# The order of dimensions in the loads of q and the stores of the result of a linear-attention and feed-forward kernel

## The chip, the cores and the metric

The kernel runs on one core of a Trainium2 chip. The metric is the device time of one execution in microseconds, the median of several runs of the same program. A separate execution is recorded by the hardware profiler, and every view in this document comes from such an execution.

The core has five instruction streams that matter here. PE multiplies matrices (PEld is its loading of the stationary operand), DVE and ACT do elementwise work, POOL only sets constants, and SP issues almost all DMA transfers. SP is a queue: it issues in program order, and an issue that has to wait holds up everything behind it. The core's 16 DMA engines carry the transfers.

## The reference

```python
kv  = einsum('bhsd,bhse->bhde', k, v)            # per batch and head, 64 x 64
out = einsum('bhsd,bhde->bhse', q, kv)
rms = sqrt(mean(out * out, axis=-1) + 1e-6)
attn = out / rms * g_norm
x = attn.transpose(0, 2, 1, 3).reshape(4608, 512)  # tokens x (heads * 64)
h = x @ w_in                                     # 512 -> 2048
g = h * tanh(softplus(h))                        # mish
result = g @ w_out                               # 2048 -> 512
```

There are 8 batches, 8 heads, 576 positions and a head size of 64, all in float32; the two weights arrive in float64 and are converted on the chip.

## The kernel before

Both large products are done by a two-by-two block scheme with seven block products instead of eight. Each float32 operand is split into a high and a low part, and three matmuls stand for one.

**Part 1** goes over nine tiles of 512 tokens (j = 0 to 8). A tile is 28 slots: four groups of seven block products, each product 12 matmuls (`mm_in`, line 480). The products of tile j run while the attention of tile j + 1 is prepared in between, at slots that a table in `attention` fixes: `steps(u, n, ...)` puts a step at slot n of the tile before. A tile's attention has two units, u = 0 and u = 1, of four heads each. A unit loads q (`load`, line 288, into the tile `qs`, which has one buffer), transposes it in 32 by 32 blocks on DVE (`transpose`, line 293), splits it (lines 118 and 119), multiplies it with the batch's k-v product (`project`, lines 316 to 321), squares, sums and normalises. The load of u = 1 is put at slot 2 and its transpose at slot 7; the load of u = 0 of the next tile is put at slot 10, and its transpose at slot 28, which is slot 0 of the tile after.

A tile of 512 tokens straddles two batches of 576 positions, so it has one or two segments (`segments`). Tokens are placed so that a partition holds neighbouring positions: a segment of L * 32 positions of one head, which is contiguous in memory, is cut into 32 runs of L positions, and the 32-block transpose turns this into columns of tokens.

Evictions of the products go to the buffers `ula`, `ulb` and `ur` (two of each), through mish, and then to the scratch `gd` in HBM (`put_in`, lines 498, 503 and 506). A buffer can only be written again (lines 443, 448 and 457, on ACT) when its store has landed. Tile 0 also contains most of the k-v products: loads of k and v at lines 212 and 213, matmuls at line 233, and the copy at line 245. The conversion of w_in (line 135 loads it) falls there too, that of w_out in tiles 1 to 7.

**Part 2** multiplies g, read back from `gd` in 18 groups of 256 tokens (`g_load`, line 687, two groups ahead), with w_out (`mm_out`, line 728). A group's result of 256 rows stands in one `ur` buffer as [128 partitions, 2, 512]: token rows r = 0 in the first half, r = 1 in the second. `o_store` (line 752) writes it out after the group's last eviction (line 757).

What the change and the prediction touch: `load` in `unit_steps`, `o_store`, and the order of SP, which is the order of the plan's slots. The wait of ACT at line 448 for a landed `gd` store and that of DVE at line 293 for `qs` are the two places where DMA timing enters part 1.

Of the kernel before, what the change touches and what calls it, by code (L numbers as in the profile page):

```python
# [26 lines left out]
def linear_attention_rms_mish_ffn(  # L27
# [34 lines left out]
    nc = tc.nc  # L62
    B, H, S, D = q.shape
    NTOK, DM = out.shape
    DF = w_in.shape[1]
    w_in, w_out = w_in.bitcast(U32), w_out.bitcast(U32)
    P = 128
    R = 32
# [8 lines left out]
    G = 2 * P  # L77
# [183 lines left out]
    def segments(j):  # L261

        n = (S - T) * j
        segs = []
        if n:
            segs.append((j - 1, S - n, slice(0, n)))
        if n < T:
            segs.append((j, 0, slice(n, T)))
        return segs
# [3 lines left out]
    def unit_steps(j, u):  # L273
        st = {}

        def load():


            t = qs[u] = att.tile([P, 2, T // R * D], F32, name="qs")
            for a in range(2):  # L280
                for o in range(2):
                    for b, s0, cols in segments(j):
                        run = (cols.stop - cols.start) // R * D
                        src = q[b, 4 * u + 2 * a + o, s0:s0 + 1, :]
                        src = bass.AP(src.tensor, src.offset, [[R, 2], [run, R], [1, run - R]])
                        c0 = cols.start // R * D
                        dst = t[o * D:(o + 1) * D, a, c0:c0 + run - R]
                        nc.sync.dma_start(dst, src)

        def transpose():  # L290
            t = att.tile([P, 2, T], F32, name="fh" if j < T32 else "fa")
# [86 lines left out]
        def normalize():  # L378
# [4 lines left out]
            else:  # L383
                nc.vector.tensor_mul(o, o, st["rr"])

        return {f.__name__: f for f in (load, transpose, halves, project, square, scaled, squares, sums, rstd, keep, spread, normalize)}


# [209 lines left out]
    for j in range(2, NF2):  # L598
        t = 3 * (j - 2)
# [3 lines left out]
    for n in range(len(order_kv) + len(staged)):  # L603
        t = n * 6 // 8
# [39 lines left out]
    for j in range(1, NT):  # L644
        r = units[j][1]["rstd"]
# [93 lines left out]
    def o_store(st):  # L739

        i, half = divmod(st["s"], T // G)
        for r in range(2):
            c0 = (half * G + r * P) // R
            for b, s0, cols in segments(i):
                first, L = cols.start // R, (cols.stop - cols.start) // R
                lo, hi = max(c0, first), min(c0 + P // R, first + L)
                if lo < hi:
                    row = b * S + s0 + lo - first
                    dst = out[row:row + 1, :]
                    dst = bass.AP(dst.tensor, dst.offset, [[DM, hi - lo], [L * DM, R], [1, DM]])  # L750
                    src = st["o"][(lo - c0) * R:(hi - c0) * R, r, :]
                    nc.sync.dma_start(dst, src)

    def put_out(st, block, bank, t):
        o = o_dst(st, block)
        if block == "21":
            nc.scalar.copy(o, bank)  # L757
            at(t + 1, lambda: o_store(st))
        else:
            nc.vector.tensor_add(o, bank, o)  # L760
# [17 lines left out]
    for i in range(NT):  # L778
        for n in range(NQ):
            st = {"i": i, "n": n, "bank": bank_new}  # L780
            t = NS * i + 7 * n
# [3 lines left out]
    t = NS * NT  # L785
# [13 lines left out]
    st = gs[0]  # L799
# [46 lines left out]
    nc.vector.tensor_add(o12, bank[S4], o12)  # L846
    nc.vector.tensor_add(o21, bank[A22], o21)
    o_store(st)


# [50 lines left out]
```

## Time and profile before

| What | us |
|---|---|
| median of 3 runs | 1190.36 (1190.31 to 1193.13) |
| profiled execution, its own time | 1194.02 |
| its span, first to last instruction | 1192.0 |
| part 1 up to the first product of tile 0 | 79.4 |
| tile 0 | 176.7 |
| tiles 1 to 6 together | 452.4 |
| tile 7 | 59.1 |
| tile 8, the last | 51.5 |
| part 2 | 373 |
| PE busy | 885.9 |
| DVE busy | 611.5 |
| ACT busy | 464.6 |

The tiles are cut at the start of the first matmul of line 480 in each tile, found in the record in order of time (each tile has 28 times 12 such matmuls). A row of the view by stretches gives, for a stretch of time, the busy time and the count of instructions of PE, PEld, DVE, ACT and POOL, then the granted clock of PE, the mean busy share of the 16 DMA engines, and the GB/s that they moved. A row of the view in order of time has the start, the length, the engine, the line, the operation, what it writes and reads, the count merged into the row, and in brackets the idle time ahead of it with what ended it. On SP the length of a row is the time from the first issue to the end of the last.

### The profile page before, as it was taken

The page shows a single profiled execution, that of the slowest core. Times are in us where ns is not written, and L with a number is a line of the kernel's source. Part 1 is how long each engine was busy: PE and PEld are TensorE (multiplying, and loading weights), DVE is VectorE, ACT ScalarE, POOL GpSimd, SP SyncE. Part 2 cuts the span into 40 slices and gives each one's busy share as a digit, 9 for nine tenths or more (in the row PEclk, how much of TensorE's full clock was granted, in tenths as well). Part 3 has the DMA queues.
Part 4 walks back from the last instruction along what each step waited for, and adds up shares of the span by engine and source line. Part 5 has one row for each costly group of instructions (what it writes and reads, how often), then busy time and mean ns, then how long its engine had stood idle before and what let it go on. Part 6 is the DMA issues. An engine that isn't in the chain of part 4 may idle for free. (4 is left out here: it accounts for less than half of the span.)

```text
span 1192.0 us, 16959 instructions
## 1 busy us (share of the span) xinstructions
PE 885.9 (74%) x6940; PEld 838.2 (70%) x6940; DVE 611.5 (51%) x801; ACT 464.6 (39%) x703; POOL 3.4 (0%) x19
## 2 busy tenths in 40 slices
PE   1341472796685756858768576979999999999997
PEld 0121362586575756748657575979999999999997
DVE  1161352354363543726426354626877676767673
ACT  0041231443443534526444254634444444343432
POOL 1000000000000000000000000000000000000000
PEclk9875696788797878978888788999999999999999
DMA  5223384752643435436352463599444434343531
GB/s 164 87 79 102 122 254 132 241 180 77 206 143 127 141 123 178 156 107 189 123 173 76 170 194 126 165 373 383 145 151 128 137 118 146 110 153 102 163 98 35
DMA packets 156092, 181.05 MB, mean 152 GB/s; under 512 B 15920, under 2 KB 135728, under 8 KB 154992
## 3 DMA queue, kind: packets, MB, share of 16 engines
q1 hardware_dynamic: 152816, 177.63, 45.8%
q10 hardware_dynamic: 3200, 2.36, 0.7%
q8 instruction: 54, 0.88, 0.3%
q14 instruction: 22, 0.18, 0.0%
HBM read 116.13 MB, written 63.83 MB: 151 GB/s over the span
## 5 line engine op out<-in xcount | busy, mean ns | idle before, releaser
L480 PE MATMUL bc<-gf,wf 128*128 128x256 f32 x1296 | 192.3, 306 | 61.2 <-ACT ur L448 54.6
L480 PEld LDWEIGHTS bc<-gf,wf 128*128 128x128 f32 x1296 | 181.4, 212 | 65.1 <-ACT ur L448 56.1
L480 PE MATMUL a<-gf,wf 128*128 128x256 f32 x1296 | 183.5, 299 | 27.0 <-ACT ur L457 13.9
L728 PE MATMUL a<-wf,gf 128*128 128x256 f32 x1632 | 201.8, 283 | 0.5 <-DVE ur L760 0.5
L728 PEld LDWEIGHTS a<-wf,gf 128*128 128x128 f32 x1632 | 198.4, 192 | 0.7 <-DVE ur L760 0.7
L480 PEld LDWEIGHTS a<-gf,wf 128*128 128x128 f32 x1296 | 173.2, 205 | 31.8 <-ACT ur L457 16.2
L119 DVE TENSOR_TENSOR gf<-g,gf 128x1024 fp32r<-128x1024 f32 (+1 forms) x123 | 132.9, 1087 | 87.9 <-ACT gf L118 87.8
L728 PE MATMUL bc<-wf,gf 128*128 128x256 f32 x1224 | 152.6, 283 | 0.1
L118 ACT CAST gf<-g 128x1024 fp32r<-128x1024 f32 (+1 forms) x123 | 114.5, 939 | 90.2 <-DVE g L708 65.1
L728 PEld LDWEIGHTS bc<-wf,gf 128*128 128x128 f32 x1224 | 149.4, 192 | 0.3 <-ACT gf L118 0.3
L448 ACT COPY ur<-bc 128x512 f32<-128x512 f32 (+1 forms) x53 | 27.4, 517 | 186.0 <-DMA gd<-ur 156.1
L233 PE MATMUL s<-vm,km 128*64 128x64 f32 x448 | 24.2, 265 | 81.6 <-DMA vm<-in_v_dram 54.9
L233 PEld LDWEIGHTS s<-vm,km 128*64 128x64 f32 x448 | 20.1, 172 | 86.3 <-DMA vm<-in_v_dram 28.6
L115 ACT ACTIVATE ur<-ur 128x1024 f32<-128x1024 f32 x36 | 38.1, 1058 | 70.8 <-DVE ur L500 70.8
L319 PE MATMUL x<-fh,kv 128*128 128x128 f32 (+7 forms) x52 | 21.3, 409 | 59.6 <-ACT fh L118 59.6
L480 PEld LDWEIGHTS a<-a,wf 128*128 128x128 f32 x432 | 56.5, 196 | 9.8 <-DVE ur L500 5.6
L480 PE MATMUL a<-a,wf 128*128 128x256 f32 x432 | 60.1, 290 | 2.5 <-DVE ur L500 2.4
L319 PEld LDWEIGHTS x<-fh,kv 128*128 128x128 f32 x52 | 13.2, 254 | 61.5 <-ACT fh L118 61.0
L293 DVE STREAM_TRANSPOSE fa<-qs 128x1024 f32<-128x1024 f32 x14 | 17.4, 1242 | 72.2 <-DMA qs<-in_q_dram 72.2
L500 DVE TENSOR_TENSOR ula<-bc,ula 128x512 f32<-128x512 f32 x36 | 24.7, 685 | 35.5 <-PE bc L480 23.3
L500 DVE TENSOR_TENSOR ur<-bc,ur 128x512 f32<-128x512 f32 x36 | 24.6, 683 | 35.0 <-PE bc L480 23.9
L118 ACT CAST gf<-gf 128x512 fp32r<-128x512 f32 x45 | 27.7, 617 | 37.6 <-DVE gf L406 18.2
(129 smaller groups left out, 927.0 us busy)
## 6 DMA issues: line engine op xcount, KB each, us to landing
g<-gd SPq DMA_DIRECT2D x18, 2048.0 KB
gd<-ur SPq DMA_DIRECT2D x36, 512.0 KB
wod<-wst SPq DMA_DIRECT2D x16, 896.0 KB
wf<-wod SPq DMA_DIRECT2D x8, 1792.0 KB
gd<-ula SPq DMA_DIRECT2D x36, 256.0 KB
gd<-ulb SPq DMA_DIRECT2D x36, 256.0 KB
w<-in_moe_w_out_dram SPq DMA_DIRECT2D x32, 256.0 KB
out_dram<-ur SPq DMA_DIRECT2D x32, 256.0 KB
```

Of the source, the lines that this page charges most:

```text
L115: nc.scalar.activation(o, i, AF.Mish)
L118: nc.scalar.copy(hi, src)
L119: nc.vector.tensor_sub(lo, src, hi.bitcast(F32))
L233: nc.tensor.matmul(kvps[o * D:(o + 1) * D, b % 2, h0 // 2 + i, :], kt, vt, start=(c == 0), stop=(c == CM))
L293: nc.vector.transpose(t.rearrange("p a (c d) -> p (a c) d", d=R), src)
L319: nc.tensor.matmul(ps[:, c], kl, qh, start=True, stop=False)
L448: then(t + 2, lambda: nc.scalar.copy(dst(st, "22"), st["c"]))
L480: nc.tensor.matmul(bank[:, jj], w[:, right, a, kc, :], xf[:, b, kc, :], start=first and jj == kc == s == 0, stop=(kc == 1 and s == 2), ski ...
L500: nc.vector.tensor_add(o, bank, o)
L728: nc.tensor.matmul(bank, gf[:, a, c, :], wo[c][:, right, b, :], start=first and c == s == 0, stop=(c == NF2 - 1 and s == 2), skip_group_ch ...
```

## The change

Both transfers move the same elements between the same places; what changes is the order of dimensions within a transfer, and how the work is cut into transfers.

In `load`, one transfer was one head of one segment: 64 partitions, with the HBM side as [2, 32, run]. Now one transfer is 32 partitions of two heads of one segment: the HBM side is [32, 2, run], and the tile's side [32 partitions, 2, run]. There are four per segment and unit before and after, with the same rows of contiguous bytes.

In `o_store`, one transfer was a half r of a group, [4 or 2, 32, 512] on the HBM side. Now it is 32 partitions with both halves, [32, 2, 512], or with one half where a batch ends within the group. In the program text this is 88 transfers of at most 128 KB instead of 40 of at most 256 KB.

```diff
-            for a in range(2):
-                for o in range(2):
-                    for b, s0, cols in segments(j):
-                        run = (cols.stop - cols.start) // R * D
-                        src = q[b, 4 * u + 2 * a + o, s0:s0 + 1, :]
-                        src = bass.AP(src.tensor, src.offset, [[R, 2], [run, R], [1, run - R]])
-                        c0 = cols.start // R * D
-                        dst = t[o * D:(o + 1) * D, a, c0:c0 + run - R]
-                        nc.sync.dma_start(dst, src)
+            for i in range(4):
+                for b, s0, cols in segments(j):
+                    run = (cols.stop - cols.start) // R * D
+                    src = q[b, 4 * u + i // 2, s0:s0 + 1, R * (i % 2):]
+                    src = bass.AP(src.tensor, src.offset, [[run, R], [2 * S * D, 2], [1, run - R]])
+                    c0 = cols.start // R * D
+                    nc.sync.dma_start(t[i * R:(i + 1) * R, :, c0:c0 + run - R], src)
...
-        for r in range(2):
-            c0 = (half * G + r * P) // R
+        for n in range(P // R):
+            c = (half * G + n * R) // R
             for b, s0, cols in segments(i):
                 first, L = cols.start // R, (cols.stop - cols.start) // R
-                lo, hi = max(c0, first), min(c0 + P // R, first + L)
-                if lo < hi:
-                    row = b * S + s0 + lo - first
+                rs = [r for r in range(2) if first <= c + r * P // R < first + L]
+                if rs:
+                    row = b * S + s0 + c + rs[0] * P // R - first
                     dst = out[row:row + 1, :]
-                    dst = bass.AP(dst.tensor, dst.offset, [[DM, hi - lo], [L * DM, R], [1, DM]])
-                    src = st["o"][(lo - c0) * R:(hi - c0) * R, r, :]
-                    nc.sync.dma_start(dst, src)
+                    dst = bass.AP(dst.tensor, dst.offset, [[L * DM, R], [P // R * DM, len(rs)], [1, DM]])
+                    nc.sync.dma_start(dst, st["o"][n * R:(n + 1) * R, rs[0]:rs[-1] + 1, :])
```

The order of SP around a load of q in tile 3 (the load of u = 1, and what is queued behind it), before:

```order
L503 DMA gd_93<-ula 128x2x256
L288 DMA qs<-in_q_dram 64x1x480 x8
L199 DMA wod_102<-wst 1792x1x128
L506 DMA gd_93<-ur 128x1024
L135 DMA w_2715<-in_moe_w_out_dram 128x2x256 x2
L498 DMA gd_93<-ulb 128x2x256
```

and now:

```order
L501 DMA gd_93<-ula 128x2x256
L286 DMA qs<-in_q_dram 32x2x480 x8
L199 DMA wod_102<-wst 1792x1x128
L504 DMA gd_93<-ur 128x1024
L135 DMA w_2715<-in_moe_w_out_dram 128x2x256 x2
L496 DMA gd_93<-ulb 128x2x256
```

Nothing has moved: the same eight issues stand at the same place, each with 32 partitions of two heads instead of 64 of one. Lines behind the change are numbered two lower.

The order of SP in part 2, where `g` is the read-back of two groups ahead and `out_dram` the result, before:

```order
L687 DMA g<-gd_92 128x16x256
L752 DMA out_dram<-ur 4x32x512 x2
L687 DMA g<-gd_93 128x16x256
L752 DMA out_dram<-ur 2x32x512 x2
L752 DMA out_dram<-ur 4x32x512
L687 DMA g<-gd_93 128x16x256
```

and now:

```order
L685 DMA g<-gd_92 128x16x256
L749 DMA out_dram<-ur 32x2x512 x4
L685 DMA g<-gd_93 128x16x256
L749 DMA out_dram<-ur 32x512 x4
L749 DMA out_dram<-ur 32x2x512 x2
L685 DMA g<-gd_93 128x16x256
```

Between two read-backs stand four to eight stores instead of two or three. Each of the stores with both halves needs both to be evicted.

## The prediction

> **What bounds the kernel now.** I read the view by stretches first, cut at the tiles.
>
> ```profile
> 0.00:79.39 79.39, 17.92 (x97) 8.60 (x97) 16.82 (x22) 14.18 (x22) 3.39 (x19) 0.85 0.36 110
> 79.39:256.09 176.70, 94.74 (x908) 78.94 (x909) 67.29 (x90) 50.39 (x77) 0.00 (x0) 0.70 0.58 177
> 256.09:708.50 452.41, 317.10 (x2211) 299.09 (x2210) 217.51 (x330) 196.09 (x308) 0.00 (x0) 0.84 0.44 143
> 708.50:767.60 59.10, 48.43 (x358) 45.10 (x358) 34.01 (x51) 31.47 (x50) 0.00 (x0) 0.91 0.45 148
> 767.60:819.05 51.45, 42.65 (x338) 42.04 (x337) 17.73 (x33) 20.87 (x38) 0.00 (x0) 0.93 0.91 336
> 819.05:1192.00 372.95, 365.04 (x3036) 364.46 (x3036) 258.12 (x278) 151.55 (x210) 0.00 (x0) 1.00 0.41 135
> ```
>
> Part 2 (last row) is PE's: 365 of 373 us busy at a granted clock of 1.00. Part 1 is nobody's. In tiles 1 to 6 (third row) PE is idle for 452.4 - 317.1 = 135.3 us, DVE and ACT are busy for less than half, and DMA for 0.44. The tiles cost 75.4 us each there, 59.1 in tile 7 and 51.5 in tile 8. Tile 7 prepares a unit with a load of q but issues none for a next tile; tile 8 has none. Something that ends with the loads of q costs some 16 us in tiles 1 to 6. The view of waits names it, in these rows for the stretch of tiles 1 to 6:
>
> ```profile
> ACT ur L448 <- DMA gd<-ur: 134.5, 12, 14.3
> DVE fa L293 <- DMA qs<-in_q_dram: 61.8, 6, 12.5
> PE x L319 <- ACT fh L118: 51.4, 6, 11.7
> PE bc L480 <- ACT ur L448: 47.5, 6, 9.0
> ```
>
> Per tile DVE waits once for q and ACT twice for a store of `ur`; PE pays 51.4 us for the first (projection waits for the split of the transposed q) and 47.5 for the second. How both hang on the load shows in tile 3, in order of time:
>
> ```profile
> 413.64 10.25 SPq L288 DMA_DIRECT2D qs<-in_q_dram  x8
> 423.99 3.88 SPq L199 DMA_DIRECT2D wod<-wst  x1
> 427.96 7.21 SPq L506 DMA_DIRECT2D gd<-ur  x1
> 436.33 1.25 DVE L293 STREAM_TRANSPOSE fa<-qs 128x1024 f32<-128x1024 f32 x1 [12.26 <-DMA qs<-in_q_dram]
> 437.85 14.63 SPq L288 DMA_DIRECT2D qs<-in_q_dram  x8
> 441.33 0.58 PE L319 MATMUL x<-fh,kv 128*128 128x256 f32 x1 [11.31 <-ACT fh L118]
> 452.58 1.73 SPq L506 DMA_DIRECT2D gd<-ur  x1
> 464.53 2.93 PE L480 MATMUL bc<-gf,wf 128*128 128x256 f32 x12 [7.12 <-ACT ur L448]
> 469.56 3.14 PE L480 MATMUL a<-gf,wf 128*128 128x256 f32 x24 [2.11 <-ACT ur L457]
> ```
>
> The load of u = 1 is issued from 413.64 and q is there at 436.33, 22.7 us later. The store of `ur` behind it takes 7.21 us to issue, until just when q has landed. The load of u = 0 (437.85) does the same: a store issued at 452.58 frees its buffer only shortly before 464.53, and PE stops for 7.12 and 2.11 us. The reason is in the view by stretches, for short ones:
>
> ```profile
> 415.00:421.00 6.00, 5.12 (x42) 5.00 (x42) 4.69 (x7) 4.16 (x8) 0.00 (x0) 1.00 0.13 41
> 429.00:431.00 2.00, 1.02 (x9) 0.81 (x7) 0.00 (x0) 0.00 (x0) 0.00 (x0) 1.00 1.03 334
> 1187.00:1190.50 3.50, 0.00 (x0) 0.00 (x0) 0.00 (x0) 0.00 (x0) 0.00 (x0) 0.70 0.23 66
> ```
>
> While q alone is moving, the DMA share is 0.13, which is 2 of 16 engines, at 41 GB/s. At 429 to 431, when the `wod` store has joined, whose outermost dimensions are multiples of 16, the share is 1.03, at 334 GB/s. At 1187 the last store of the result, with an outermost dimension of 4, is alone: 0.23, some 4 of 16. So the engines used follow the outermost dimension (2, 4, many), and whatever else is queued has a sixteenth of itself on each of the two engines that q keeps busy: it lands when q is through.
>
> **The change, part by part.** *q's loads.* A unit is 8 transfers of 120 KB, 983 KB. At the 334 GB/s of 16 engines this takes 2.9 us instead of 20. An issue that nothing holds up takes some 0.6 us:
>
> ```profile
> 84.17 0.59 SPq L212 DMA_DIRECT2D vm<-in_v_dram  x1
> 88.14 11.99 SPq L288 DMA_DIRECT2D qs<-in_q_dram  x8
> ```
>
> so 8 issues take 8 * 0.6 = 4.8 us instead of 10 to 15, and q is there some 8 us after the first issue (4.8, 0.4 for the last transfer's drain, and some 2 us of latency: the last store of the result, shown below, lands 5.8 us after its issue starts, of which 4 are drain), where DVE waited from 424.07, 10.4 us after it. Both stops per tile go. The other stores have only 4.8 us of issues ahead of them on SP, the one new lateness I allow for.
>
> Tiles 1 to 6: the PE waits of 51.4 and 47.5 us go, and the one of line 457 that follows (2.11 in tile 3, so some 12 in six): 111 us. That leaves 341 us. The clock adds: it was 0.84 here and 0.91 in tile 7 with one stop of the two, so 317.1 us of busy PE become 317.1 * 0.84 / 0.91 = 293, another 24. I take 315 us, a gain of 137. Bounds: 111 without the clock; and 166 if PE never idles at tile 8's clock (317.1 * 0.84 / 0.93 = 286). DVE (36 us a tile) and ACT (33) have no room in the stops that they lose, since both idled through them, and fit in 52.5 us.
>
> [...]
>
> Tile 7 has the first stop alone: 8.2 us of PE by its row of waits plus a little clock, 9.5 us (bounds 8 and 11).
>
> ```profile
> PE x L319 <- ACT fh L118: 8.2, 1, 8.2
> ```
>
> Tile 0: three loads of q, and behind each of them k and v late by the same mechanism:
>
> ```profile
> 120.71 1.02 PE L233 MATMUL s<-vm,km 128*64 128x64 f32 x14 [25.44 <-ACT kv L245]
> 144.60 0.69 PE L233 MATMUL s<-vm,km 128*64 128x64 f32 x8 [15.76 <-DMA vm<-in_v_dram]
> 204.21 0.59 PE L233 MATMUL s<-vm,km 128*64 128x64 f32 x6 [21.48 <-DMA vm<-in_v_dram]
> 118.78 10.20 SPq L288 DMA_DIRECT2D qs<-in_q_dram  x8
> ```
>
> The stops are 62.7 us together, but DMA becomes the limit: 0.58 of 176.7 is 102 us of all 16 engines, and the highest share of the stretches above is 0.91, so 113 us is the least. I take 125, at a share of 0.82: a gain of 52. Bounds 64 and 19; the smaller is SP's own time alone (11.99, 10.20 and about as much for the third, less 4.8 each).
>
> Start: DVE waits for q twice, and projection behind it.
>
> ```profile
> 35.40 1.25 DVE L293 STREAM_TRANSPOSE fh<-qs 128x1024 f32<-128x1024 f32 x1 [13.81 <-DMA gf<-in_moe_w_in_dram]
> 60.97 1.25 DVE L293 STREAM_TRANSPOSE fh<-qs 128x1024 f32<-128x1024 f32 x1 [15.99 <-DMA qs<-in_q_dram]
> ```
>
> The releaser in the first row is the last semaphore seen; the transpose reads only `qs`. Both go: 29.8 us at most. The weights and k and v of the start share the engines with q, so I take 24 (bounds 30 and 12).
>
> *The result's stores.* In part 2 there are 48 more issues, 48 * 0.54 = 26 us of SP. What hides them is SP's own waiting there:
>
> ```profile
> SPq L687 <- DVE gf L119: 151.2, 15, 10.2
> SPq L752 <- ACT ur L757: 109.1, 17, 8.6
> SPq L896 <- DMA out_dram<-ur: 5.2, 1, 5.2
> 1185.16 0.54 SPq L752 DMA_DIRECT2D out_dram<-ur  x1
> ```
>
> Read-backs wait 151 us for their buffer and stores 109 for the last eviction. Without this cover the 26 us would be in the time. PE waits for no store there, so spreading them over 16 engines gains nothing but at the end. There SP waits 5.2 us for the last store, 256 KB on 4 engines. Now all 512 KB stand behind the last eviction, in four issues: three issues later (1.7 us), but the drain falls from 4 us (256 KB at 66 GB/s) to 0.4 for the last 128 KB. That is a gain of 2 us (bounds 0 and 3).
>
> Sum: 137 + 9.5 + 52 + 24 + 2 = 224.5. The profiled execution took 1194.0, so 969.5; it was 3.7 us above the median, so **965 us**. With all small bounds (111 + 8 + 19 + 12 + 0 = 150) it is 1040, with all large ones (166 + 11 + 64 + 30 + 3 = 274) 916.
>
> **The rivals.** *The store of `ur` stays late.* In tile 3 it stands behind a `wod` store that waits for a conversion (3.88 us in the row at 423.99), and eight issues of q still stand ahead of it. If this alone makes ACT wait, the second stop stays: 47.5 + 12 us of PE and half the clock, so 965 + 72 = 1037. Against it: tile 7, with the same stores and no load for a next tile, has no such wait of PE in its row of 59.1, and 7.21 us of issue end with q.
>
> *Too few engines.* No row shows what an outermost 32 gives; 2 gave 2, 4 gave 4. If 32 partitions went to 4 engines, a load would take 983 KB at 4/16 of 334 GB/s, 11.8 us: 9 more than forecast, of which DVE's 10.4 us of head start hide nearly all in the first stop. With 4 us a tile left over, some 6 for each load in tile 0 and 12 at the start it is about 965 + 24 + 18 + 12 = 1019. If it changes nothing at all, 1190. [...]
>
> *Slower.* q's rows could cost far more on 16 engines that read the same two heads and write the same 32 partitions at once. Now a load would hold all engines instead of two, and all else waits for it in full. A tile has 0.44 * 75.4 = 33 us of transfers, 28 of them not q's. With two loads of more than 24 us it needs over 48 + 28 = 76, and is slower than now; that is a packet of about eight times its present length. At 30 us a load six tiles gain 6 * 12.6 = 76 us, tile 0 some 10, the start some 10: about 1285. Against it: 16 engines moved 334 GB/s at 429 us with two of them on q.
>
> **How the numbers follow.** Forecast 0.82, late store 0.08, four engines 0.05, no effect 0.03, slower 0.02. The forecast's own range is 916 to 1040, which holds the first two rivals' times as well; I give 915 to 1040. Runs of this kernel lie within 0.3% of each other, so a change under that (3.6 us) is none: faster 0.95, same 0.03, slower 0.02.
>
> **What would show it.** In the changed profile, stretches with q alone have a DMA share well over 0.13; eight issues of q take about 5 us; the waits of line 293's transpose for `qs` and of line 448 for `gd` shrink to a few us per tile; tiles 1 to 6 are even at 50 to 55 us, tile 7 near 50, tile 8 and part 2 as before; the end after the last eviction is 2 us shorter. Wrong it would be if the wait of line 448 keeps its size with q's wait gone, if tile 0 stays over 155 us, or if tiles settle above 57, which would mean a chain through DVE and ACT that the stops had hidden.

## The result

The changed kernel takes 958.34 us (median, 957.17 to 959.49), the kernel before 1190.34 beside it: a ratio of 0.805, 95% interval 0.803 to 0.8071. The forecast was 965 us, with a range of 915 to 1040.

The view by stretches, cut at the same places (start, tile 0, tiles 1 to 6, tile 7, tile 8, part 2), of the changed kernel:

```profile
0.00:47.77 47.77, 17.05 (x97) 8.40 (x97) 16.72 (x22) 14.20 (x22) 3.39 (x19) 0.85 0.71 183
47.77:176.66 128.89, 95.59 (x909) 79.55 (x910) 67.22 (x90) 50.26 (x77) 0.00 (x0) 0.78 0.85 242
176.66:485.37 308.71, 284.56 (x2210) 271.55 (x2209) 215.30 (x329) 194.37 (x307) 0.00 (x0) 0.98 0.70 209
485.37:535.41 50.04, 47.55 (x358) 44.94 (x357) 34.76 (x53) 31.86 (x50) 0.00 (x0) 0.97 0.60 181
535.41:587.12 51.71, 43.54 (x339) 42.94 (x337) 17.85 (x33) 21.01 (x38) 0.00 (x0) 0.90 0.91 334
587.12:957.70 370.58, 365.04 (x3036) 364.46 (x3036) 258.11 (x278) 151.50 (x210) 0.00 (x0) 1.00 0.44 136
```

All of the gain but some 2 us is ahead of tile 8. In tiles 1 to 6 PE is idle for 308.7 - 284.6 = 24 us instead of 135, and its clock rose from 0.84 to 0.98; its busy time fell by 32.5 us with it. The tiles are even, 49 to 55 us each.

The same place in tile 3 as before the change, in order of time (DVE's transposes of u = 0 and u = 1, and SP):

```profile
286.55 1.24 DVE L291 STREAM_TRANSPOSE fa<-qs 128x1024 f32<-128x1024 f32 x1
287.81 3.63 SPq L286 DMA_DIRECT2D qs<-in_q_dram  x8
291.54 0.57 SPq L199 DMA_DIRECT2D wod<-wst  x1
292.21 1.30 SPq L504 DMA_DIRECT2D gd<-ur  x1
...
298.16 1.23 DVE L291 STREAM_TRANSPOSE fa<-qs 128x1024 f32<-128x1024 f32 x1
299.42 3.97 SPq L286 DMA_DIRECT2D qs<-in_q_dram  x8
303.78 0.35 SPq L504 DMA_DIRECT2D gd<-ur  x1
```

Eight issues take 3.6 to 4.0 us instead of 10 to 15, the store of `ur` behind them 1.30 and 0.35 instead of 7.21 and 1.73, and the second transpose starts with no idle time ahead of it, 10.4 us after the first issue. Three stretches in which q moves, by the view by stretches:

```profile
197.20:200.00 2.80, 2.80 (x26) 2.80 (x26) 1.38 (x2) 1.83 (x3) 0.00 (x0) 1.00 0.77 212
288.50:291.50 3.00, 2.12 (x17) 1.89 (x17) 1.99 (x4) 1.59 (x4) 0.00 (x0) 1.00 0.81 229
300.00:303.00 3.00, 3.00 (x28) 3.00 (x27) 2.52 (x4) 2.98 (x7) 0.00 (x0) 1.00 1.03 293
```

The share is 0.77, 0.81 and 1.03, where it was 0.13. In the first two stretches SP issues nothing but q (196.23 to 199.85, 287.81 to 291.44); in the third other transfers move too. Of the two waits that carried the argument, the one of DVE for `qs` in tiles 1 to 7 is gone. The other is left in tile 8 alone, where it was before, and where no q is loaded; the rows are of the waits of the whole run and of tile 8, after:

```profile
ACT ur L446 <- DMA gd<-ur: 12.2, 2, 9.9
PE bc L478 <- ACT ur L446: 7.4, 1, 7.4
```

and the row of tile 8 before, for comparison:

```profile
PE bc L480 <- ACT ur L448: 7.1, 1, 7.1
```

The end: SP now waits 1.7 us for the last stores, after four issues in 1.74 us.

```profile
953.23 1.74 SPq L749 DMA_DIRECT2D out_dram<-ur  x4
SPq L893 <- DMA out_dram<-ur: 1.7, 3, 0.9
```

The 5.2 us of wait and 0.54 of issue became 1.7 and 1.74, a gain of 2.3 us.

### The profile page after: what moved, and what is told of

Read it like the earlier page. It is cut to its first block, busy times and chain, and to the rows that moved or that the text cites. A ratio compares the mean times of both kernels' runs of the same rounds, so it can differ in the third digit from the quotient of the medians.

```text
span 957.7 us, 17048 instructions
## 1 busy us (share of the span) xinstructions
PE 853.3 (89%) x6940; PEld 811.8 (85%) x6940; DVE 610.0 (64%) x801; ACT 463.2 (48%) x703; POOL 3.4 (0%) x19
## 4 chain that ended last, share of the span: by engine, by line
PE 62%; DMA 12%; DVE 11%; ACT 7%; SPq 4%; issue 3%; ACTq 0%; DVEq 0%
PE a L726 20%; PE bc L726 15%; PE a L478 11%; PE bc L478 7%; DMA vm<-in_v_dram 3%; DMA gd<-ula 3%; PE q L808 2%; PE s L233 2%; DMA w<-in_moe_w_in_dram 2%; DMA gd<-ur 2%; DMA qs<-in_q_dram 2%; DVE ur L498 1%; DVE fl L119 1%; ACT gf L118 1%; SPq L135 1%
## 5 line engine op out<-in xcount | busy, mean ns | idle before, releaser
L478 PE MATMUL a<-gf,wf 128*128 128x256 f32 x1296 | 179.9, 295 | 17.2 <-DVE gf L380 10.9
L478 PE MATMUL bc<-gf,wf 128*128 128x256 f32 x1296 | 176.8, 291 | 15.0 <-DVE ula L498 7.6
L478 PEld LDWEIGHTS a<-gf,wf 128*128 128x128 f32 x1296 | 169.3, 201 | 21.7 <-issue 11.7
L478 PEld LDWEIGHTS bc<-gf,wf 128*128 128x128 f32 x1296 | 167.1, 197 | 17.5 <-issue 9.0
L233 PE MATMUL s<-vm,km 128*64 128x64 f32 x448 | 24.3, 266 | 32.7 <-DMA vm<-in_v_dram 20.7
L118 ACT CAST gf<-a 128x1024 fp32r<-128x1024 f32 x17 | 17.9, 1051 | 53.4 <-DVE a L703 53.4
L119 DVE TENSOR_TENSOR gf<-gf 128x512 fp32r<-128x512 f32 x45 | 31.0, 689 | 17.3 <-ACT gf L118 16.7
L455 ACT COPY ur<-a 128x512 f32<-128x512 f32 (+1 forms) x53 | 27.4, 517 | 30.2 <-PE a L726 24.6
L119 DVE TENSOR_TENSOR fl<-fa,fh 128x1024 fp32r<-128x1024 f32 x28 | 34.1, 1219 | 9.4 <-ACT fh L118 9.4
```

The costliest lines, as they stand in the source:

```text
L118: nc.scalar.copy(hi, src)
L119: nc.vector.tensor_sub(lo, src, hi.bitcast(F32))
L233: nc.tensor.matmul(kvps[o * D:(o + 1) * D, b % 2, h0 // 2 + i, :], kt, vt, start=(c == 0), stop=(c == CM))
L455: then(t + 4, lambda: nc.scalar.copy(dst(st, "12"), st["a"]))
L478: nc.tensor.matmul(bank[:, jj], w[:, right, a, kc, :], xf[:, b, kc, :], start=first and jj == kc == s == 0, stop=(kc == 1 and s == 2), ski ...
```

## The experiments

A time without an interval is that of a single run. Runs of one kernel lay up to 0.8% apart (945.19 to 952.80 us in the widest case), so a difference of up to some 8 us between single runs can be chance.

**The two edits apart.** `e_loads` has the change of `load` alone, `e_stores` that of `o_store` alone (the diffs are the two halves of the change).

> Only q's loads are changed, the result's stores are as before. Theory (loads of q on 2 of 16 engines made all of the loss in part 1, stores only the end): 960 us, the 958.3 of the whole change plus the 2 us at the end; part 1 as in the whole change, last store waited for 5 us. Rival (the stores' 4 engines also cost something in part 2, or their 88 issues do): over 965 or under 956.

> Only the result's stores are changed, q's loads are as before. Theory: 1188 us, 2 us under the kernel before, all of it after the last eviction. Rival (the stores carry part of the 232 us): under 1180; rival (48 more issues on SP show in part 2): over 1192.

The loads alone: 959.18 us, ratio 0.8055 (0.8021 to 0.8089). The stores alone: 1188.80 us, ratio 0.9977 (0.9963 to 0.9991), 2.6 us under the kernel before. The loads carry nearly all of it; the stores are worth some 2 us at the end. In the loads alone those 2 us do not stand out from the spread of its runs (955.92 to 962.96). That the last wait is the stores' shows in the profile, with the stores as before (first row) and with their change alone (second):

```profile
SPq L894 <- DMA out_dram<-ur: 5.1, 1, 5.1
```

```profile
SPq L895 <- DMA out_dram<-ur: 1.7, 3, 0.9
```

**One stop at a time.** Of the changed kernel, some loads go back to the old form.

```diff
+            if j >= 3 and u == 0:       # e_u0_old;  e_u1_old: j >= 2 and u == 1
+                (the loops of before)
+            else:
                 (the loops of the change)
```

> The changed kernel, but the loads of unit u = 0 of tiles 3 to 8 (issued in tiles 1 to 6 at slot 10, needed 18 slots later) in the form of before, on 2 engines. Theory (the two busy engines make the stores behind the load late, and ACT waits for a buffer of ur): the second stop comes back in tiles 1 to 6, 47.5 + 12 us of PE and some 12 of clock: 1030 us, with some 12 us waits of ACT at the copy to ur for a store to gd. Rival (all of the loss was q itself coming late to its transpose): 958 to 962, since this load has 18 slots of at least 1.44 us, 26 us, to land in 23.

> The changed kernel, but the loads of unit u = 1 of tiles 2 to 8 (issued in tiles 1 to 7 at slot 2, needed at slot 7) in the form of before. Theory: the first stop comes back in tiles 1 to 7, 51.4 + 8.2 us of PE and some 14 of clock: about 1030 us; DVE waits for q some 10 to 12 us seven times, tile 7 is back at 59 us, tiles 1 to 6 at about 62. Rival (the first stop is only felt with the second): under 990.

Old loads for u = 0: 1035.08 us, tiles 1 to 6 back at 384.7 from 308.7. Old loads for u = 1: 1037.86 us, tiles 1 to 6 at 377.4 and tile 7 at 58.8. The first is the sharper one, since q was never late there. In tile 3 of it the old load of u = 0 is issued, in the new form's place:

```profile
325.36 13.28 SPq L289 DMA_DIRECT2D qs<-in_q_dram  x8
338.74 1.73 SPq L515 DMA_DIRECT2D gd<-ur  x1
350.74 2.93 PE L489 MATMUL bc<-gf,wf 128*128 128x256 f32 x12 [8.05 <-ACT ur L457]
355.78 4.29 PE L489 MATMUL a<-gf,wf 128*128 128x256 f32 x24 [2.11 <-ACT ur L466]
```

No transpose of tiles 1 to 6 waits for q there; the waits of that stretch are ACT's for a store of `ur` and PE's for ACT:

```profile
ACT ur L457 <- DMA gd<-ur: 71.6, 6, 15.3
PE bc L489 <- ACT ur L457: 51.6, 6, 11.2
```

So half of the loss in the tiles was paid at a place that does not wait for q. Two things make that store late in tile 3, and no run separates them. SP is held up by the load, so the store's issue starts 13.4 us after the first issue of q, where it is 4.4 in the changed kernel. And its buffer is free 11.4 us after that, where such a store lands in 5.1 (median) in the changed kernel.

With u = 1 old, the transpose waits for q seven times, ACT as often for a store of `ur`, and PE behind them:

```profile
ACT ur L457 <- DMA gd<-ur: 70.5, 7, 13.8
DVE fa L302 <- DMA qs<-in_q_dram: 69.9, 7, 12.1
PE x L328 <- ACT fh L118: 57.5, 7, 11.3
```

The first row belongs to the first stop too, and the same holds for the kernel before. In ACT's rows a copy to `ur` stands ahead of the split that PE waits for. Here is tile 3 before, where q had been transposed at 437.58:

```profile
439.75 0.59 ACT L448 COPY ur<-bc 128x512 f32<-128x512 f32 x1 [13.55 <-DMA gd<-ur]
440.23 1.05 ACT L118 CAST fh<-fa 128x1024 fp32r<-128x1024 f32 x1
```

In all seven tiles before, the split starts right behind that copy, 0.1 to 3.2 us after the end of the transpose. So q and the store of `ur` are late together in the first stop. The third buffer for `ur`, below, shows q's part: without ACT's wait, the first stop is still 42.4 of 51.4 us.

The two stops add up: 76.7 + 79.5 = 156 us over the changed kernel's 958.3, and tiles 1 to 7 lost 511.5 - 358.8 = 153 us with both.

**How many engines.** Each of q's transfers is cut once more along its 32 partitions, into 16 + 16, 25 + 7 or 31 + 1.

```diff
-                    nc.sync.dma_start(t[i * R:(i + 1) * R, :, c0:c0 + run - R], src)
+                    for r0, r1 in ((0, M), (M, R)):      # M = 16, 25 or 31
+                        part = bass.AP(src.tensor, src.offset + r0 * run, [[run, r1 - r0], [2 * S * D, 2], [1, run - R]])
+                        nc.sync.dma_start(t[i * R + r0:i * R + r1, :, c0:c0 + run - R], part)
```

> The changed kernel with each load of q cut once more, into 16 + 16 partitions: twice the issues, still an outermost dimension that 16 divides. Theory (engines decide, issues only where SP is full): 16 issues take some 7 us instead of 4, hidden in tiles 1 to 7, felt at the start and in tile 0, where SP issues without a gap: 958 + 4 to 15, so 962 to 973. Rival (what the change gained was fewer or larger pieces, not engines): some 40 us more, 1000.

> As the cut into 16 + 16, but into 25 + 7 partitions. [...] Theory: a load lasts 9 to 12 us instead of 5, which DVE's 10 us of head start still hides in tiles 1 to 7; start and tile 0 lose 5 us for each of 5 loads: 975 to 1000. Rival (stops grow in proportion to the load's length): a third of the 232 us back, 1035. [...]

> [...] Theory (q's engine is the bottleneck): 983 KB at 21 to 24 GB/s is 41 to 47 us a load, two loads a tile, 82 to 95 us for each of tiles 1 to 6, so about 1350 us, slower than the kernel before, with a DMA share of 0.06 while q alone moves. Rival (partitions, not engines, set the pace): as the cut into 16 + 16, under 980.

| pieces | us | start | tile 0 | tiles 1 to 6 | tile 7 |
|---|---|---|---|---|---|
| 32, as changed | 958.34 | 47.8 | 128.9 | 308.7 | 50.0 |
| 16 + 16 | 990.53 | 52.3 | 142.7 | 321.9 | 48.7 |
| 25 + 7 | 991.13 | 57.4 | 137.7 | 322.6 | 49.4 |
| 31 + 1 | 1511.97 | 115.0 | 227.3 | 669.6 | 75.8 |

Stretches with hardly anything but q, by the view by stretches, first of 25 + 7, then of 31 + 1:

```profile
312.00:317.00 5.00, 5.00 (x44) 5.00 (x43) 3.69 (x6) 4.33 (x8) 0.00 (x0) 1.00 0.35 123
```

```profile
210.00:211.00 1.00, 0.00 (x0) 0.00 (x0) 0.00 (x0) 0.00 (x0) 0.00 (x0) 0.50 0.07 28
```

0.35 is 5.6 of 16 engines, and 0.07 is 1.1. That 25 + 7 would run on five to seven engines and 31 + 1 on one was my assumption, which no run had shown then; the 9 to 12 us and the 41 to 47 us of a load stood on it. At the 123 GB/s of the first row 983 KB take 8 us, an estimate. With 31 + 1, at about one engine, the kernel is far slower than the kernel before, as expected, and by more than the 1350 us: tiles 1 to 6 take 112 us each where two loads of 41 to 47 us were to set 82 to 95. Tile 3 shows what that sum left out:

```profile
571.09 31.83 SPq L288 DMA_DIRECT2D qs<-in_q_dram  x16
611.70 1.25 DVE L293 STREAM_TRANSPOSE fa<-qs 128x1024 f32<-128x1024 f32 x1 [30.19 <-DMA qs<-in_q_dram]
613.36 35.51 SPq L288 DMA_DIRECT2D qs<-in_q_dram  x16
657.98 2.93 PE L480 MATMUL bc<-gf,wf 128*128 128x256 f32 x12 [25.83 <-ACT ur L448]
681.72 33.32 SPq L288 DMA_DIRECT2D qs<-in_q_dram  x16
```

The first load takes 40.6 us to its transpose, as expected, and the second and what is queued behind it some 44. But the next load is not issued when the second is through. The tile `qs` has one buffer, and DVE transposes the second load out of it only in its own slot, at 680.45. That is another 24 us.

The surprise is that 25 + 7 costs no more than 16 + 16: five to six engines are enough here. A load on them has to end within DVE's 10.4 us of head start, and in tiles 1 to 7 it does (DVE waits for q once in that run, 5.6 us for `fh`, and never for the `fa` of these tiles); the start is 5 us longer than with 16 + 16, and tile 0 is 5 us shorter. What both have in common is twice the issues, for smaller pieces, and both are some 32 us over the change. That missed the expected 962 to 973 us for 16 + 16 and is nearer to the rival's 1000; no run has smaller pieces without more issues. With 16 + 16 the start and tile 0 are 18.3 us longer, close to five loads at the 3.6 us that eight more issues take. That the added issues of SP are the cost there is argued from this sum alone. In tiles 1 to 6, which take 306.6 to 308.7 us in every run with q's new loads uncut, it is 13.2 more, where I had put nothing: there 16 issues hold SP for 7.3 us, and ACT's wait for a store of `ur` begins to come back. The rows are the load in the order of time and the wait in the whole run (in the changed kernel it is 12.2 us in two waits, both in tile 8):

```profile
376.68 7.33 SPq L288 DMA_DIRECT2D qs<-in_q_dram  x16
ACT ur L448 <- DMA gd<-ur: 20.6, 5, 9.7
```

In tiles 1 to 6 alone it is 11.0 us in four waits, and PE's wait behind it (for ACT's copy to `ur` at line 457) grows from 3.1 to 10.2 us. So it is the rival of the late store, with the issues of q as the likely cause, and accounts for some 7 of the 13 us. At 3.6 us of issues the cover holds, at 7.3 it does not quite.

**A third buffer for `ur`, in the kernel before.**

```diff
+    u3 = part1.enter_context(tc.tile_pool(name="u3", bufs=1))
...
-            st[name] = up.tile([P, 2, shape], F32, name="u" + name)
+            third = name == "r" and st["i"] < NT - 1 and (NQ * st["i"] + st["n"]) % 3 == 2
+            st[name] = (u3 if third else up).tile([P, 2, shape], F32, name="u" + name)
```

> The kernel before, with a third buffer for ur in part 1 (every third group takes it, up to tile 7); loads and stores as before. Theory (the second stop is ACT waiting for a buffer whose store is stuck on the two engines): the third buffer gives 7 slots, some 11 us, more, so the waits at the copy to ur of 10 to 14 us nearly go, and PE's 47.5 + 12 us with them: 1120 us, with DVE's 12 us waits for q unchanged. Rival (the stuck stores of ula and ulb, or SP itself, stop ACT next): over 1170.

1177.80 us: the rival's time, and its kind of cause, though mostly not the transfers that it named. Tiles 1 to 6 took 436.1 us instead of 452.4. ACT's wait for `ur` is gone from them. In its place ACT waits for other transfers behind a load of q: five times for the read-back of the k-v product (third row), twice for the store of `wod` (12.3 us) and once for a store of `ula` (5.7 us). PE stops behind them:

```profile
DVE fa L294 <- DMA qs<-in_q_dram: 60.0, 6, 12.3
PE x L320 <- ACT fh L119: 42.4, 6, 8.5
ACT kv L119 <- DMA kvr<-kvd: 29.2, 5, 9.0
PE a L481 <- DVE ur L502: 22.5, 5, 8.0
```

What SP issued behind a load of q came late here, whichever of these transfers it was, so a buffer more at one place mostly moved the stop.

**What sets tile 0 now.** For long stretches SP issues there with hardly a gap, as in the first two rows, of the changed kernel. But it also waits for PE's k-v products to free its buffers, by the third row:

```profile
75.01 0.59 SPq L212 DMA_DIRECT2D vm<-in_v_dram  x1
75.65 0.61 SPq L213 DMA_DIRECT2D vr<-in_v_dram  x1
SPq L212 <- PE s L233: 28.9, 8, 21.3
```

Three kernels give some of its issues to GpSimd's queue: the small loads of k and v (`e_krpool`, line 213), all loads of k and v (`e_kvpool`), or q's (`e_qpool`).

```diff
-            eng.dma_start(r, src[b, hs, SM:S, :].rearrange("h p d -> p h d"))
+            (nc.gpsimd if b else eng).dma_start(r, src[b, hs, SM:S, :].rearrange("h p d -> p h d"))   # e_krpool
-            staged.append((b, h0, kv_load(nc.sync, ...
+            staged.append((b, h0, kv_load(nc.gpsimd, ...                                              # e_kvpool
-                    nc.sync.dma_start(t[i * R:(i + 1) * R, ...
+                    (nc.gpsimd if j else nc.sync).dma_start(t[i * R:(i + 1) * R, ...                  # e_qpool
```

> The changed kernel, with the loads of the last 64 positions of k and v (52 of the 176 issues of tile 0) issued from GpSimd's queue, which is idle, instead of SP's. Theory (tile 0 of the changed kernel is set by SP, which issues there without a gap for 80 us at 0.6 us each): tile 0 falls from 129 us by up to 52 * 0.6 = 31 us, bounded by DMA at a share of 0.92 (0.85 * 129 = 110 us of transfers, 119 us): 948 us. Rival (DMA or PE's chain sets tile 0): 955 to 962; rival (GpSimd's issues land later): over 962.

> As the one with 52 issues, but all loads of k and v of batches 1 to 7 (104 to 112 issues) from GpSimd's queue. Theory as there, with the same DMA bound: 945 to 950 us. Rival (GpSimd issues more slowly than 1.1 us each, 112 * 1.1 = 123 us, and becomes the limit of tile 0): 960 to 990.

> The changed kernel with q's loads of tiles 1 to 8 from GpSimd's queue. Theory (stores still stand 4 us behind q's issues on SP in tiles 1 to 7, but nothing waits for it): tiles 1 to 7 unchanged within 1 us each, tile 0 faster by at most 3 * 4 us: 948 to 958. Rival (SP's order still costs in the tiles): under 940; rival (GpSimd's issues are slow enough to make q late at slot 7): over 965.

> The kernel with the last positions of k and v loaded through GpSimd's queue, timed in rounds. Theory (7 us of tile 0 are SP's issues): 951 to 953 us, a ratio of 0.798 to 0.801 to the kernel before, under the 0.805 of the change and of the loads alone. Rival (the one look was chance): a ratio of 0.803 to 0.807.

The small loads: 951.97 us in a single run and a median of 951.12 in six, ratio 0.7966 (0.7941 to 0.7991), clear of the change's 0.803 to 0.8071. Tile 0 takes 122 us instead of 128.9, the rest is unchanged. All loads of k and v (104 issues): 980.65 us, tile 0 at 147.0, in the range of its rival. There PE waits for `vm` 47.3 us instead of 20.7. GpSimd's issues take 0.67 us each, not 1.1, but its rows show idle time ahead of many issues that no semaphore in the profile explains:

```profile
PE s L233 <- DMA vm<-in_v_dram: 47.3, 16, 5.9
POOL vm L212 <- issue: 26.2, 19, 4.3
POOL km L212 <- issue: 20.8, 11, 4.0
```

Why GpSimd stops there stays open. q's loads from GpSimd: 958.17 us, no change, so q's 3.6 us on SP cost nothing that shows in tiles 1 to 7 (308.2 and 50.0 us) and little in tile 0 (128.1). Taking 52 issues from SP saved 7 us of tile 0, not the 31 that SP's own time would give. So SP is a part of what sets tile 0, and what the rest is stays open; the DMA share was 0.85 in both.

## Why the prediction was right

By the profiled executions, 1194.02 and 959.49 us:

| Term | gain forecast, us | measured |
|---|---|---|
| start | 24 | 31.6 |
| tile 0 | 52 | 47.8 |
| tiles 1 to 6 | 137 | 143.7 |
| tile 7 | 9.5 | 9.1 |
| tile 8 | 0 | -0.3 |
| part 2 and the end | 2 | 2.4 |
| sum of the spans | 224.5 | 234.3 |

**Tiles 1 to 6.** The mechanism stood as told: two engines, and a stop for q and a stop for what was queued behind q. That each of q's two engines holds a sixteenth of what is queued is an estimate from the share of 1.03 with the `wod` store (16 engines, evenly); the views do not tell the engines apart. The runs with one load at a time priced the first at 80 us, with tile 7, and the second at 77, and the one with u = 0 showed the second without any wait for q. One reading was too simple: the first stop was put down to q alone, but a late store of `ur` ended at the same place, and some 9 of its 51.4 us were the store's by the run with a third buffer. As both came from the loads, the sum did not suffer.

Of the two terms, PE's idle time fell by the 111 us that were forecast. The sum came out some 7 us too small by its clock term: PE's busy time fell by 32.5 us, not 24. I scaled it to tile 7's clock of 0.91, but tile 7 still had a stop in it; without either it is 0.98. The scaling is also too coarse: with 0.98 it would have given 45 us. So that this term was near was partly luck.

**Start.** This is the one term outside its own bounds (12 to 30 us), for two reasons. I took 6 us off the two waits for what shares the engines with q, and that was not needed: 0.59 us of wait are left. And I took the two waits as all there was. But ACT's own queue, which issues the first loads of k and v, issued the last of them at 15.28 us before and at 11.79 after, so that ACT's first instruction and after it DVE's came earlier too. That q's load had held that queue up is likely, but no run shows it alone. The rows are ACT's wait before and after the change, and DVE after:

```profile
ACT L531 <- DMA gf<-in_v_dram: 15.9, 1, 15.9
```

```profile
ACT L529 <- DMA ula<-in_v_dram: 12.4, 1, 12.4
```

```profile
14.88 0.69 DVE L145 TENSOR_SCALAR fl<-fl 128x1024 uint32<-128x1024 uint32 x1 [14.88 <-ACT fl L140]
18.01 1.24 DVE L291 STREAM_TRANSPOSE fh<-qs 128x1024 f32<-128x1024 f32 x1
27.77 1.25 DVE L291 STREAM_TRANSPOSE fh<-qs 128x1024 f32<-128x1024 f32 x1 [0.59 <-DMA qs<-in_q_dram]
```

DVE began at 18.37 before, and its transposes were at 35.40 and 60.97. The 3.5 us between 14.88 and 18.37, the same as ACT's 15.9 less 12.4, are what the two waits of 29.8 us did not contain. The second transpose came 33.2 us earlier, of which the start kept 31.6.

**Tile 0.** The size was right (125 forecast, 128.9), the reason only in part: I gave DMA as the limit, at a share of 0.82; it reached 0.85, but moving issues off SP shortened the tile as well.

**The end and part 2.** As forecast; the 48 more issues cost nothing that shows, since PE's busy time and the rest of part 2 are the same.

**The rivals.** The late store did not stay, but 16 issues in place of 8 brought some of it back, so its cover is thin. Too few engines did not happen: with nothing but q issued the share was 0.77 and 0.81, where four of 16 would be 0.25. That 32 partitions would run on four engines, the term of this rival, no run shows. What it would have cost was probably overrated: 25 + 7, at five to six engines, took 991.13 us and 16 + 16 took 990.53; four were not tried. Slower did not happen: with nothing but q issued the rate is 212 GB/s at a share of 0.77 and 229 at 0.81, where the `wod` store with q on two engines had 334 at 1.03. That is far from eight times.

## What to carry to other kernels

In this kernel a DMA share of 0.13 while q alone moved was two of 16 engines, and it went with the outermost dimension: 2 had 0.13, 32 had 0.77 and 0.81, 25 + 7 had 0.35 and 31 + 1 had 0.07. The five to six engines of 25 + 7 did as well as 16 + 16 here (991.13 and 990.53 us). About half of the price (76.7 of 156 us, by the runs with one load at a time) was paid by other transfers, queued behind it, so look at the waits of unrelated buffers before adding buffers to them. And count the issues when a transfer is cut to use more engines: doubling them here gave back a seventh of what the engines had gained.

## What was not expected of the hardware

The issue of a transfer of q in the changed kernel takes 0.45 us (3.63 for 8, with the gaps between them). On two engines it takes 0.59, counted the same way over the first four of the load at 413.64 before. The next three take some 2.2 us each, and all eight 10 to 15. With 31 + 1 it is 31 to 36 for 16 (30.77 at 456.27, 35.51 at 613.36). That the load itself holds the issues up is the likely reason: 120 KB take 2.4 to 3.0 us, an estimate from the 41 and 51 GB/s of q alone at 415 to 421 and 422 to 427 before.
